# Attention into a routed expert layer: V splits, query/key halves, low parts and the router's last chunks moved in the order of the steps

## The chip, the cores and the metric

The kernel runs on one core of one Trainium2 chip. The metric is the device time of one execution in microseconds (us). TensorE (PE), VectorE (DVE), ScalarE (ACT), GpSimd (POOL) and SyncE (SP) each run their own instructions in order. SyncE only issues DMAs here, and GpSimd issues some.

## What is computed

Three stages follow each other. Cluster-masked attention over batch 2, 8 heads, 768 positions, 64 channels; then a router that sends each of the 1536 tokens (of 512 channels) to one of 8 experts; then a feed-forward layer of width 2048.

```python
    mask = q_assign[:, :, :, None] == k_assign[:, :, None, :]
    scores = scale * np.matmul(q, k.transpose(0, 1, 3, 2))
    scores = np.where(mask, scores, -1000000000.0)
    scores = scores - np.max(scores, axis=-1, keepdims=True)
    attn = np.exp(scores)
    attn = attn / (np.sum(attn, axis=-1, keepdims=True) + 1e-09)
    return np.matmul(attn, v).astype(np.float32)
...
    e_idx = np.argmax(logits, axis=1)
...
        h = np.maximum(x[mask] @ w1[e], 0.0)
        ye = h @ w2[e]
        out[mask] = gate_w[mask, None] * eom[mask, e, None] * ye
...
    h = x @ w_in
    g = h * (1.0 / (1.0 + np.exp(-h)))
    return (g @ w_out).astype(np.float32)
```

`q_assign` and `k_assign` are each position's nearest of 16 centroids.

## The kernel before

Attention is cut into 96 steps: 8 periods of 12. A period is one pair of heads of one batch entry, and its steps are 2 heads times 6 tiles of 128 queries. `run` goes through iterations i = 0, 1, 2, ... and writes each engine's instructions in the order of that loop; its last lines chain every instruction to the one before it on its engine, so that the order written is the order run.

Iteration i does this, in this order: the scores of step i + 1 (`qk_mm`, L371 and L373); what was deferred (`flush`: copies out of PSUM and DMAs); for a step i - 2 on TensorE its high part (`high`, ScalarE, L424); the softmax of step i (`soft`: VectorE's reduction L392, ScalarE's exponential L394, and, where the step is not on TensorE, the copy to 16 bits, L403); the eviction of a finished group of outputs (`out`, L469 to L471); the low part of a TensorE step i - 2 (`low2`, VectorE, L429); the transposes of a TensorE step i - 1 (`turn`, L418) or the low part of any other step i - 1 (`low`, GpSimd's subtraction L438); the first half of the tasks that are due in this round; up to two PVs (`pv`, L462 to L464, seven iterations behind their scores); the second half of the tasks; and one or two chunks of the router.

A probability tile is used as two 16-bit parts, high and low, and must be transposed. There are two ways. **TensorE steps** (chosen in `onpe`, in pairs) are transposed by TensorE into two PSUM tiles, from which ScalarE takes the high part and VectorE the low part. **The other steps** make both parts in SBUF, and for two steps together SyncE issues a DMA transpose (L442, tile pt). For steps 4, 5 and 8 of a period the 16-bit copy is VectorE's cast L437, which is written in `low`. PSUM tiles of `turn`, of the query/key transposes (L178), of the cluster scores (L193), of the masks and of the router share three banks.

**Tasks** come from a table of rounds in `plan` (round r is iteration r of the period; period 0 has its own rounds, marked z). They prepare the next pair's heads: transposes of queries and keys (`tr`), whose second halves are copied to other partitions by DMA (L298: QB from QA issued by GpSimd, KB from KA by SyncE); cluster scores and the best cluster (`sc`, and `best` in three pieces, L203 to L211, VectorE); masks (`m`: L338, L339, and four DMAs of SyncE, L342). They also split V into high and low (`split_v`, GpSimd, L152 to L156) and the queries and keys of the pair after the next (`halves`, ScalarE L330 and GpSimd L331).

SyncE issues, in the order of the loop, the loads of queries and keys (L169), the DMA transposes, the copies and stores of zeros (L1195). GpSimd also issues the router's scatters (L772). The router (`s.router`, L680 to L772) is a generator: one chunk of it is run in an iteration, a chunk that works on the PSUM banks only where no TensorE step needs them. Its part for a group of query tiles starts one iteration after the group's eviction was written (`late`). After the last step the rest of it is run without steps in between, and the first expert reads what was scattered (L905, tile xst to xt).

Of the kernel before, what the change touches and what calls it, by code (L numbers as in the profile page):

```python
# [30 lines left out]
class Att:  # L31
# [224 lines left out]
    def plan(s, pi, pairs, g0=None, vg=None):  # L256

        nc = s.nc
        u = []
        add = lambda r, f: u.append((r, f))  # L260
        nx = lambda g: lambda: next(g, None)
        if pi + 2 < len(pairs):
            add(3 if g0 else -1, lambda: s.load_qk(*pairs[pi + 2]))
        z = bool(g0)
        b, hp = pairs[pi]
        sp = lambda h, b=b, hp=hp: lambda: s.split_v(b, 2 * hp + h)
        if z:
            for r in (-1, 0, 0, 1, 1):
                add(r, nx(g0))
            for r in (3, 4, 4, 5, 6, 7, 8, 8):  # L270
                add(r, nx(vg))
        for h, r in enumerate((9, 10) if z else (-1, 0)):
            add(r, sp(h))
        if pi == 1:
            s.v1 = s.load_v(1)
        for r in {1: (3, 6, 10), 2: (6, 10), 3: (4, 5, 6, 6)}.get(pi, ()):
            add(r, nx(s.v1))
        if pi + 1 < len(pairs):
            b, hp = pairs[pi + 1]
            if z:  # L280
                for r in range(2):
                    add(r, lambda r=r: s.halves(pairs[1], r))
            hd = [None, None]
            ch = [None, None]
            oh = []

            def start(j):
                hd[j] = s.heads(2 * hp + j, j)
                if j == 0:
                    oh.append(s.ohp.tile([128, NT, 2, 2, C], BF16, tag='oh', name='oh'))  # L290

            def tr(j, a, half):
                if a == 0 and half == 0:
                    start(j)
                s.turned(hd[j][1 + 2 * a], s.nqk[b, hp][a], j, half, (-0.125, 1.0)[a])
                if half:
                    src, dst, e = ((hd[j][1][0:64], hd[j][2][0:64], nc.gpsimd), (hd[j][3][64:128], hd[j][4][0:64], nc.sync))[a]
                    s.defer.append(lambda: e.dma_start(dst.bitcast(F32), src.bitcast(F32)))  # L298

            def sc(j):  # L300
                s.scores(hd[j])
                ch[j] = s.best(s.clb, oh[0], j)
            bst = lambda j: lambda: next(ch[j])
            tr8 = [(j, a, half) for j in range(2) for a in range(2) for half in range(2)]
            for (j, a, half), r in zip(tr8, (2, 2, 3, 3, 4, 4, 5, 5) if z else (-1, -1, -1, 0, 0, 0, 3, 3)):
                add(r, lambda j=j, a=a, half=half: tr(j, a, half))
            for j, (r, r1, r2, r3) in enumerate(((4, 5, 6, 7), (6, 7, 8, 9)) if z else ((1, 2, 3, 4), (4, 5, 6, 7))):
                add(r, lambda j=j: sc(j))
                for q in (r1, r2, r3):
                    add(q, bst(j))  # L310

            def m():
                s.masks(oh[0], hd)
                for j in range(2):
                    s.ready[b, hp, j] = hd[j]
            add(9 if z else 8, m)
        if pi + 2 < len(pairs):
            for i, r in enumerate((5, 6) if not z else (9, 10)):
                add(r, lambda i=i: s.halves(pairs[pi + 2], i))
        u.sort(key=lambda x: x[0])  # L320
        return u
# [54 lines left out]
    def onpe(s, st):  # L376
        g = st['i'] // 2
        n = len(s.steps) // 2

        return (g % 3 == 0 and g >= 6) or g >= n - 6  # L380

    def dve(s, st):

# [65 lines left out]
    def pv(s, st):  # L449
        nc = s.nc  # L450
        b = st['b']
        h = st['hd'][0]
        t = st['t']
        pt = st['pt']
        g = st['g']
        gl = slice(g[0], g[-1] + 1)
        if t == g[0]:
            s.o = s.T('o2')[:, :NT * (D + 2)].rearrange('p (t d) -> p t d', t=NT) if st['j'] and st['pi'] == 7 and (g[-1] == NT - 1) else s.ps_o.tile([128, NT, D + 2], F32, tag='o', name='o')
        o = s.o
        vh, vl = s.vh[b, h]  # L460
        for kt in range(NT):
            nc.tensor.matmul(o[:, t, 0:D + 2], lhsT=pt[:, 0, kt], rhs=vh[:, kt], start=kt == 0, stop=False)  # L462
            nc.tensor.matmul(o[:, t, 0:D], lhsT=pt[:, 0, kt], rhs=vl[:, kt], start=False, stop=False)  # L463
            nc.tensor.matmul(o[:, t, 0:D + 2], lhsT=pt[:, 1, kt], rhs=vh[:, kt], start=False, stop=kt == NT - 1)  # L464
        if t == g[-1]:
            def ev():
                n = len(g)
                rs = s.sm.tile([128, NT], F32, tag='rs', name='rs')[:, :n]
                nc.vector.tensor_scalar(rs, o[:, gl, D], 1e-09, s.inv[b][:, 0, h:h + 1], op0=ALU.add, op1=ALU.mult)  # L469
                nc.vector.reciprocal(rs, rs)  # L470
                nc.vector.tensor_tensor(s.xb[b][:, gl, h * D:(h + 1) * D], o[:, gl, 0:D], rs.unsqueeze(2).to_broadcast([128, n, D]), op=ALU.mult)  # L471
                if h % 2 and s.router:
                    s.late.append((s.now + 1, b, h // 2, g))
            s.oev = ev

    def run(s):
# [36 lines left out]
        rg = []  # L513
        free = False
        n = len(steps)
        done = 0
        i = -1
        base = 0
        todo = []
        while done < n:  # L520
            s.now = i
            if i + 1 < n:
                st = steps[i + 1]
                if (i + 1) % (2 * NT) == 0:
                    base = i + 1
# [10 lines left out]
            if 0 <= i < n:  # L536
                s.soft(steps[i])
            s.out()
            if 2 <= i < n + 2 and s.onpe(steps[i - 2]):
                s.low2(steps[i - 2])  # L540
            if 1 <= i < n + 1:
                (s.turn if s.onpe(steps[i - 1]) else s.low)(steps[i - 1])
            now = []
            while todo and todo[0][0] <= i - base:
                now.append(todo.pop(0)[1])
            for f in now[:len(now) // 2]:
                f()
            for k in range(3 if i >= n - 12 else 2):
# [5 lines left out]
                f()  # L554
            if s.late and i >= s.late[0][0]:
                rg.append(s.router(s, *s.late.pop(0)[1:]))
            for k in range(2):
                if rg and (k == 0 or (i - base) % 12 == 9 and i < n - 12) and (free or not (1 <= i < n - 12 and s.onpe(steps[i - 1]))):
                    x = next(rg[0], 0)
                    free = x == 'free'  # L560
                    if x == 0:
                        rg.pop(0)
# [661 lines left out]
```

## Time and profile before

| | |
|---|---|
| Time, median of 3 runs | 864.39 us (862.42 to 864.69) |
| The profiled execution | 858.08 us, of which the span is 856.0 us |
| Mean granted TensorE clock in it | 0.925 |
| Busy: TensorE, VectorE, ScalarE, GpSimd | 749.6, 501.9, 415.2, 328.6 us |
| DMA | 117.09 MB, mean 137 GB/s |

The span runs from the first instruction to the last; the time has some 2 us around it. A busy share says how much of the span an engine worked, not whether it was waited for. Attention's steps take the first third of the span, the experts and the feed-forward layer the rest.

### The profile page before, as it was taken

What the parts mean: (1) busy time and instruction counts of PE and PEld (TensorE: products, weight loads), DVE (VectorE), ACT (ScalarE), POOL (GpSimd) and SP (SyncE); (2) the same over time, 40 slices, a digit from 0 to 9 for tenths busy, and PEclk for the clock granted to TensorE, in tenths of its full rate; (3) what the DMA queues carried; (4) which work ended last, traced back from release to release, by engine and by line L of the source; (5) the groups of instructions that cost most, each with busy time, mean ns of one, the idle gap of its engine ahead of it and who ended that gap; (6) DMA issues with size and microseconds to landing.
All of it is one profiled execution on the core that took longest, in us unless ns stands there. A gap on an engine that the chain in (4) does not pass through costs nothing.

```text
span 856.0 us, 14041 instructions
## 1 busy us (share of the span) xinstructions
PE 749.6 (88%) x5416; PEld 636.4 (74%) x5416; DVE 501.9 (59%) x905; ACT 415.2 (48%) x659; POOL 328.6 (38%) x271
## 2 busy tenths in 40 slices
PE   5859897869799873999899999889899999999994
PEld 4649787868788863888797887567688788878883
DVE  6757688567867777475555687699932322232221
ACT  3756777557485654565444654465522322222221
POOL 1678758385685316644333454335400000000000
PEclk9658999789799985999999999979999999999997
DMA  4399999696676536688664864465400100010001
GB/s 150 65 221 243 205 183 155 134 184 126 136 169 129 121 112 231 217 305 267 210 212 156 295 215 152 172 227 172 148 1 1 49 1 1 0 50 1 1 0 52
DMA packets 135752, 117.09 MB, mean 137 GB/s; under 512 B 100823, under 2 KB 106967, under 8 KB 135680
## 3 DMA queue, kind: packets, MB, share of 16 engines
q1 hardware_dynamic: 131728, 107.06, 48.0%
q0 software_dynamic: 3952, 9.08, 3.7%
q8 instruction: 44, 0.72, 0.4%
q14 instruction: 28, 0.23, 0.1%
HBM read 71.67 MB, written 18.45 MB: 105 GB/s over the span
## 4 chain that ended last, share of the span: by engine, by line
PE 33%; DMA 5%; issue 5%; DVE 4%; POOL 2%; ACT 1%; ACTq 0%; POOLq 0%; DVEq 0%
PE op L1146 13%; PE hp L1158 13%; PE yp L965 3%; DMA x<-ys,f 3%; PE hp L948 2%; POOL w L852 2%; PE hr L930 2%; DMA stage<-in_moe_w_out 1%; DVE stage L1091 1%; DVE stage L1092 1%; DVE stage L1090 1%; DMA stage<-in_moe_w_in 1%; DMA stage<-in_moe_w 1%; DMA out_x<-os 0%; ACT w L847 0%
## 5 line engine op out<-in xcount | busy, mean ns | idle before, releaser
L852 POOL TENSOR_TENSOR w<-stage,w 128x512 fp32r<-128x512 f32 (+1 forms) x54 | 102.2, 1898 | 117.6 <-ACT w L847 115.8
L1158 PE MATMUL hp<-XH,w 128*128 128x512 f32 x384 | 128.5, 406 | 6.8 <-DVE sg L1166 5.6
L847 ACT ACTIVATE w<-stage 128x1024 fp32r<-128x1024 f32 (+1 forms) x104 | 96.4, 940 | 62.4 <-DVE stage L1092 29.9
L438 POOL TENSOR_TENSOR p<-p,p 128x768 f16<-128x768 f32 x60 | 98.4, 1650 | 72.7 <-DVE p L437 42.3
L392 DVE TENSOR_REDUCE m<-sp 128x1 f32<-128x768 f32 x96 | 91.0, 952 | 44.4 <-PE sp L373 35.3
L394 ACT ACTIVATE p<-sp,m 128x768 f32<-128x768 f32 x96 | 86.6, 902 | 54.1 <-DVE m L392 49.3
L1146 PE MATMUL op<-w,GH 128*128 128x512 f32 x384 | 111.7, 397 | 0.0
L1166 DVE TENSOR_TENSOR sg<-hp,sg 128x512 f32<-128x512 f32 x48 | 33.1, 689 | 118.2 <-ACT sg L1165 118.2
L948 PEld LDWEIGHTS hp<-X,w 128*128 128x128 f32 x672 | 86.8, 190 | 11.4 <-DVE HL L951 7.7
L948 PE MATMUL hp<-X,w 128*128 128x256 f32 x672 | 90.0, 284 | 4.6 <-DVE HL L951 4.2
L1158 PEld LDWEIGHTS hp<-XH,w 128*128 128x128 f32 x384 | 73.9, 193 | 26.1 <-DVE sg L1166 7.2
L852 DVE TENSOR_TENSOR w<-stage,w 128x1024 fp32r<-128x1024 f32 x50 | 70.8, 1426 | 28.5 <-ACT w L847 25.1
L462 PE MATMUL o<-vh,pt 128*128 128x66 f16 x576 | 67.7, 202 | 22.2 <-DMA pt<-p 15.9
L1165 ACT ACTIVATE sg<-hp 128x512 f32<-128x512 f32 x48 | 28.6, 597 | 119.5 <-PE hp L1158 118.5
L1146 PEld LDWEIGHTS op<-w,GH 128*128 128x128 f32 x384 | 73.3, 191 | 17.5
L1158 PE MATMUL hp<-XL,w 128*128 128x512 f32 x192 | 77.6, 404 | 2.6 <-DVE XL L852 2.6
L462 PEld LDWEIGHTS <-pt 128*128 128x128 f16 x576 | 55.9, 102 | 29.8 <-DMA pt<-p 17.5
L371 PE MATMUL sp<-KA,QA 128*128 128x384 f32 x192 | 65.8, 426 | 11.8 <-ACT p L394 11.4
L463 PE MATMUL o<-vl,pt 128*128 128x64 f16 x576 | 67.1, 198 | 0.8 <-POOL vl L156 0.8
L1146 PE MATMUL op<-w,GL 128*128 128x512 f32 x192 | 67.0, 399 | 0.6 <-DVE GL L852 0.5
L464 PE MATMUL o<-vh,pt 128*128 128x66 f16 x576 | 66.9, 199 | 0.0
L965 PE MATMUL yp<-w,HH 128*128 128x512 f32 x224 | 63.7, 399 | 0.3 <-ACT HH L950 0.3
(206 smaller groups left out, 1447.2 us busy)
## 6 DMA issues: line engine op xcount, KB each, us to landing
stage<-in_moe_w SPq DMA_DIRECT2D x72, 512.0 KB, 4.7
stage<-in_moe_w_in SPq DMA_DIRECT2D x16, 512.0 KB, 4.7
stage<-in_moe_w_out SPq DMA_DIRECT2D x16, 512.0 KB, 3.5
xst<-z SPq DMA_DIRECT2D x16, 258.0 KB, 3.2
xt<-xst SPq DMA_DIRECT2D x7, 516.0 KB, 4.0
vt<-in_v SPq DMA_DIRECT2D x4, 768.0 KB, 7.2
xt<-x SPq DMA_DIRECT2D x6, 512.0 KB, 5.2
out_x<-os SPq DMA_DIRECT2D x12, 256.0 KB, 2.4
```

Source lines behind the costliest of these rows:

```text
L392: st['min'] = nc.vector.tensor_reduce(m, sv, axis=AX.XY, op=ALU.min).ins
L394: st['exp'] = nc.scalar.activation(p32, sv, AF.Exp, bias=m, scale=-1.0).ins
L438: s.nc.gpsimd.tensor_sub(p16[:, 1], p32, p16[:, 0])
L462: nc.tensor.matmul(o[:, t, 0:D + 2], lhsT=pt[:, 0, kt], rhs=vh[:, kt], start=kt == 0, stop=False)
L463: nc.tensor.matmul(o[:, t, 0:D], lhsT=pt[:, 0, kt], rhs=vl[:, kt], start=False, stop=False)
L464: nc.tensor.matmul(o[:, t, 0:D + 2], lhsT=pt[:, 1, kt], rhs=vh[:, kt], start=False, stop=kt == NT - 1)
L847: s.nc.scalar.activation(hi, src, AF.Copy)
L852: (eng or s.nc.vector).tensor_sub(lo, src, hi)
L948: nc.tensor.matmul(hp, lhsT=W1[k][w][:, f * 128:(f + 1) * 128], rhs=x[:, k, :N], start=n == 0, stop=n == 11)
L965: nc.tensor.matmul(yp, lhsT=h[:, f, i * 128:(i + 1) * 128], rhs=w, start=n == 0, stop=n == 23)
L1146: nc.tensor.matmul(op[i], lhsT=g[:, i * 128:(i + 1) * 128], rhs=w, start=f == 0 and m == 0, stop=f == 15 and m == 2)
L1158: nc.tensor.matmul(hp, lhsT=I[k, f // 8][w][:, fs], rhs=x[:, k], start=n == 0, stop=n == 11)
```

## The change

Numbers of rounds in the table of tasks are changed: in period 0 the pieces of loading V, the V splits, the second head's `best` and the halves; in all other periods the V splits go from rounds -1 and 0 to 1 and 2, and the halves from 5 and 6 to 7 and 8. `onpe` takes in one pair more, steps 6 and 7 (38 TensorE steps for 36, and 29 DMA transposes for 30). Where the step behind a TensorE step is not one itself, `low2` is written last of its iteration, as the last of the tasks. The router's part for the last evictions starts in the same iteration, and in the last iterations up to six of its chunks are run one behind the other, each with a flush.

```diff
@@ -267,9 +267,9 @@
         if z:
             for r in (-1, 0, 0, 1, 1):
                 add(r, nx(g0))
-            for r in (3, 4, 4, 5, 6, 7, 8, 8):
+            for r in (3, 3, 4, 4, 5, 6, 6, 6):
                 add(r, nx(vg))
-        for h, r in enumerate((9, 10) if z else (-1, 0)):
+        for h, r in enumerate((7, 9) if z else (1, 2)):
             add(r, sp(h))
         if pi == 1:
             s.v1 = s.load_v(1)
@@ -304,7 +304,7 @@
             tr8 = [(j, a, half) for j in range(2) for a in range(2) for half in range(2)]
             for (j, a, half), r in zip(tr8, (2, 2, 3, 3, 4, 4, 5, 5) if z else (-1, -1, -1, 0, 0, 0, 3, 3)):
                 add(r, lambda j=j, a=a, half=half: tr(j, a, half))
-            for j, (r, r1, r2, r3) in enumerate(((4, 5, 6, 7), (6, 7, 8, 9)) if z else ((1, 2, 3, 4), (4, 5, 6, 7))):
+            for j, (r, r1, r2, r3) in enumerate(((4, 5, 6, 7), (7, 8, 8, 9)) if z else ((1, 2, 3, 4), (4, 5, 6, 7))):
                 add(r, lambda j=j: sc(j))
                 for q in (r1, r2, r3):
                     add(q, bst(j))
@@ -315,7 +315,7 @@
                     s.ready[b, hp, j] = hd[j]
             add(9 if z else 8, m)
         if pi + 2 < len(pairs):
-            for i, r in enumerate((5, 6) if not z else (9, 10)):
+            for i, r in enumerate((7, 8) if not z else (8, 10)):
                 add(r, lambda i=i: s.halves(pairs[pi + 2], i))
         u.sort(key=lambda x: x[0])
         return u
@@ -377,7 +377,7 @@
         g = st['i'] // 2
         n = len(s.steps) // 2
 
-        return (g % 3 == 0 and g >= 6) or g >= n - 6
+        return (g % 3 == 0 and g > 0) or g >= n - 6
 
     def dve(s, st):
 
@@ -470,7 +470,7 @@
                 nc.vector.reciprocal(rs, rs)
                 nc.vector.tensor_tensor(s.xb[b][:, gl, h * D:(h + 1) * D], o[:, gl, 0:D], rs.unsqueeze(2).to_broadcast([128, n, D]), op=ALU.mult)
                 if h % 2 and s.router:
-                    s.late.append((s.now + 1, b, h // 2, g))
+                    s.late.append((s.now + (s.now < len(s.steps) - 2), b, h // 2, g))
             s.oev = ev
 
     def run(s):
@@ -536,13 +536,17 @@
             if 0 <= i < n:
                 s.soft(steps[i])
             s.out()
-            if 2 <= i < n + 2 and s.onpe(steps[i - 2]):
+            late = 2 <= i < n + 2 and s.onpe(steps[i - 2])
+            if late and (i - 1 >= n or s.onpe(steps[i - 1])):
                 s.low2(steps[i - 2])
+                late = False
             if 1 <= i < n + 1:
                 (s.turn if s.onpe(steps[i - 1]) else s.low)(steps[i - 1])
             now = []
             while todo and todo[0][0] <= i - base:
                 now.append(todo.pop(0)[1])
+            if late:
+                now.append(lambda st=steps[i - 2]: s.low2(st))
             for f in now[:len(now) // 2]:
                 f()
             for k in range(3 if i >= n - 12 else 2):
@@ -554,8 +558,10 @@
                 f()
             if s.late and i >= s.late[0][0]:
                 rg.append(s.router(s, *s.late.pop(0)[1:]))
-            for k in range(2):
-                if rg and (k == 0 or (i - base) % 12 == 9 and i < n - 12) and (free or not (1 <= i < n - 12 and s.onpe(steps[i - 1]))):
+            for k in range(2 if i < n - 2 else 6):
+                if i >= n - 2:
+                    s.flush()
+                if rg and (i >= n - 2 or k == 0 or (i - base) % 12 == 9 and i < n - 12) and (free or not (1 <= i < n - 12 and s.onpe(steps[i - 1]))):
                     x = next(rg[0], 0)
                     free = x == 'free'
                     if x == 0:
```

SyncE in period 0, before, from the transpose of steps 2 and 3 on (pt from p_404; p_463 is that of steps 4 and 5, p_533 of 6 and 7, p_593 of 8 and 9; the rows of L342 are the mask copies of the next pair):

```order
L442 DMA_TRANSPOSE pt<-p_404 128x24x128
L1195 DMA xst<-z 128x516
L298 DMA KB<-KA 64x768
L442 DMA_TRANSPOSE pt<-p_463 128x24x128
L1195 DMA xst<-z 128x516
L442 DMA_TRANSPOSE pt<-p_533 128x24x128
L1195 DMA xst<-z 128x516
L342 DMA QB<-mk 16x768
L342 DMA KB<-mk 16x768
L342 DMA QB<-mk 16x768
L342 DMA KB<-mk 16x768
L442 DMA_TRANSPOSE pt<-p_593 128x24x128
```

SyncE at the same place after the change (p_464 is the transpose of steps 4 and 5, p_607 of 8 and 9, and L1201 is the same store):

```order
L442 DMA_TRANSPOSE pt<-p_404 128x24x128
L1201 DMA xst<-z 128x516
L298 DMA KB<-KA 64x768
L442 DMA_TRANSPOSE pt<-p_464 128x24x128
L1201 DMA xst<-z 128x516
L342 DMA QB<-mk 16x768
L342 DMA KB<-mk 16x768
L342 DMA QB<-mk 16x768
L342 DMA KB<-mk 16x768
L442 DMA_TRANSPOSE pt<-p_607 128x24x128
```

The transpose of steps 6 and 7 and one store are gone from ahead of the four mask copies; the store comes behind the next transpose instead.

VectorE in rounds 7 to 9 of period 2, before (L392 the steps' reductions, L429 the low parts of the TensorE steps 6 and 7, L437 the cast of step 8):

```order
L392 TENSOR_REDUCE m<-sp 128x1
L429 TENSOR_TENSOR pt<-ptp,pt 128x384 x2
L392 TENSOR_REDUCE m<-sp 128x1
L429 TENSOR_TENSOR pt<-ptp,pt 128x384 x2
L437 CAST p_1752<-p_1750 128x768
L392 TENSOR_REDUCE m<-sp 128x1
```

The same place after:

```order
L392 TENSOR_REDUCE m<-sp 128x1
L429 TENSOR_TENSOR pt<-ptp,pt 128x384 x2
L392 TENSOR_REDUCE m<-sp 128x1
L437 CAST p_1767<-p_1765 128x768
L429 TENSOR_TENSOR pt<-ptp,pt 128x384 x2
L392 TENSOR_REDUCE m<-sp 128x1
```

The cast of step 8 now stands ahead of the low part of step 7.

GpSimd at the border of periods 2 and 3, before (L438 the low parts of steps 10 and 11, L152 to L156 a V split, L298 the copies of the second halves of the queries):

```order
L438 TENSOR_TENSOR p_1848<-p_1846,p_1848 128x768
L152 MEMSET vh 128x6x2
L154 TENSOR_SCALAR vt_339<-vt_339,vsc_597 128x384
L155 CAST vh<-vt_339 128x6x64
L156 TENSOR_TENSOR vl<-vt_339,vh 128x384
L298 DMA QB<-QA 64x768
L438 TENSOR_TENSOR p_1848<-p_1887,p_1848 128x768
L152 MEMSET vh 128x6x2
L154 TENSOR_SCALAR vt_339<-vt_339,vsc_597 128x384
L155 CAST vh<-vt_339 128x6x64
L156 TENSOR_TENSOR vl<-vt_339,vh 128x384
L298 DMA QB<-QA 64x768
```

The same place after:

```order
L438 TENSOR_TENSOR p_1865<-p_1863,p_1865 128x768
L298 DMA QB<-QA 64x768
L438 TENSOR_TENSOR p_1865<-p_1904,p_1865 128x768
L298 DMA QB<-QA 64x768
L152 MEMSET vh 128x6x2
L154 TENSOR_SCALAR vt_339<-vt_339,vsc_548 128x384
L155 CAST vh<-vt_339 128x6x64
L156 TENSOR_TENSOR vl<-vt_339,vh 128x384
L152 MEMSET vh 128x6x2
L154 TENSOR_SCALAR vt_339<-vt_339,vsc_548 128x384
L155 CAST vh<-vt_339 128x6x64
L156 TENSOR_TENSOR vl<-vt_339,vh 128x384
```

The two V splits stood before and behind the low part of step 11 and now stand together behind it; the second copy QB from QA comes ahead of both.

On ScalarE at the end of attention, the router's copy of 512 columns (L682) stood between the high parts of the last two steps, and its exponentials (L728, L739) behind them; these three now come ahead of both high parts.

## Rows read from the trace of the kernel before

**Rows 1.** The page, busy time and share of each engine.

```profile
PE 749.6 (88%) x5416; PEld 636.4 (74%) x5416; DVE 501.9 (59%) x905; ACT 415.2 (48%) x659; POOL 328.6 (38%) x271
```

**Rows 2.** Busy time by stretch: TensorE, its loads, VectorE, ScalarE, GpSimd; clock, DMA.

```profile
36.00:96.00 60.00, 46.70 (x499) 41.13 (x498) 42.22 (x82) 36.49 (x56) 44.66 (x39) 0.80 1.09 224
...
130.00:152.00 22.00, 15.11 (x198) 14.38 (x198) 16.59 (x32) 15.15 (x25) 18.98 (x19) 0.89 1.10 171
...
345.00:380.00 35.00, 34.62 (x229) 30.98 (x228) 21.79 (x29) 20.25 (x29) 20.30 (x12) 1.00 0.74 252
```

**Rows 3.** Timeline of TensorE: start, duration, line, count, idle time before.

```profile
62.56 0.98 PE L373 MATMUL sp<-KB,QB 80*128 80x384 f32 x2 [3.43 <-DMA KB<-mk]
...
151.81 0.24 PE L462 MATMUL o<-vh,pt 128*128 128x66 f16 x1 [6.84 <-DMA pt<-p]
...
190.77 0.24 PE L462 MATMUL o<-vh,pt 128*128 128x66 f16 x1 [7.29 <-DMA pt<-p]
...
230.78 0.62 PE L371 MATMUL sp<-KA,QA 128*128 128x384 f32 x2 [2.98 <-ACT p L394]
...
262.42 0.20 PE L462 MATMUL o<-vh,pt 128*128 128x66 f16 x1 [1.80 <-DMA pt<-p]
...
308.62 0.52 PE L418 MATMUL ptp<-ident,p 128*128 128x128 f32 x3 [1.18 <-DVE pt L429]
...
333.77 0.47 PE L905 MATMUL etp<-ident,xt 128*128 128x128 f32 x1 [13.01 <-DMA xt<-xst]
```

**Rows 4.** Timelines of SyncE and of ScalarE in period 0.

```profile
55.29 3.68 SPq L442 DMA_TRANSPOSE pt<-p  x1
...
59.68 0.59 SPq L342 DMA_DIRECT2D QB<-mk  x1
...
53.74 0.90 ACT L339 ACTIVATE mk<-mp,mcol 64x768 fp32r<-64x768 bf16 x1 [0.50 <-PE mp L338]
```

**Rows 5.** Groups of instructions in attention: count, busy time, mean ns, idle before.

```profile
L418 PE MATMUL ptp<-ident,p 128*128 128x128 f32 x216 | 32.8, 285 | 4.4 <-DVE pt L429 4.3
...
L206 DVE TENSOR_TENSOR cl<-cl,mx 128x192 f32<-128x192 f32 x14 | 5.1, 367 | 0.5
```

**Rows 6.** Timeline of SyncE at the border of periods 2 and 3.

```profile
130.22 4.32 SPq L442 DMA_TRANSPOSE pt<-p  x1
...
138.23 6.83 SPq L442 DMA_TRANSPOSE pt<-p  x1
```

**Rows 7.** Timelines of VectorE and of GpSimd there.

```profile
125.31 1.02 DVE L429 TENSOR_TENSOR pt<-ptp,pt 128x384 f16<-128x384 f32 x2 [1.61 <-ACT pt L424]
126.25 0.55 DVE L437 CAST p<-p 128x768 f16<-128x768 f32 x1
...
139.59 0.58 POOL L298 DMA_DIRECT2D QB<-QA  x1
```

**Rows 8.** Timelines of GpSimd and of SyncE at the border of periods 5 and 6.

```profile
249.00 0.12 POOL L152 MEMSET vh<- 128x12 f16 x1
...
252.48 1.67 POOL L438 TENSOR_TENSOR p<-p,p 128x768 f16<-128x768 f32 x1
...
254.18 3.62 SPq L442 DMA_TRANSPOSE pt<-p  x1
```

**Rows 9.** Timelines of VectorE and of GpSimd in the router's work.

```profile
226.54 1.67 DVE L757 TENSOR_TENSOR slot<-r_sl,r_sk 128x6 int32<-128x6 f32 x1
...
226.37 1.83 POOL L331 TENSOR_TENSOR nq<-qld,nq 128x768 fp32r<-128x768 f32 x1
```

**Rows 10.** Timelines of TensorE, VectorE and GpSimd at the end of attention.

```profile
315.85 0.23 PE L734 MATMUL rk<-moe_oh,ones 128*128 128x27 bf16 x3
...
315.92 0.29 DVE L471 TENSOR_TENSOR xb<-o,rs 128x128 f32<-128x128 f32 x1
...
321.96 0.17 DVE L761 RECIPROCAL xb<-r_g 128x2 f32<-128x2 f32 x1
...
326.74 0.98 POOL L772 DMA_INDIRECT xst<-xb,slot  x1 [0.30 <-issue]
```

## The prediction

> **What bounds the kernel now.** I read the busy shares first: TensorE is busy for 88% of the span, the three other compute engines for 38% to 59% [rows 1]. A share over the span hides two stages. Behind attention, with the experts, TensorE is full: 34.62 of 35 us at the full clock [rows 2]. Nothing that starts there can start earlier than attention ends, so what attention gains or loses is carried to the end nearly one for one. In attention TensorE is not full: from 36 to 96 us it works 46.70 of 60 us, from 130 to 152 us 15.11 of 22, with a granted clock of 0.80 and 0.89 and the DMA engines asked for more than they can move at once (share 1.09 and 1.10) [rows 2]. So the next view is TensorE's timeline, for its idle time and what ended it [rows 3]. The long waits are few: 3.43 us for the mask rows of the next keys (KB from mk), 6.84 and 7.29 us for a DMA transpose (pt), 2.98 us for an exponential, 1.80 us for another transpose, some of 1.18 us for a PSUM bank that VectorE's low part still reads, and 13.01 us ahead of the first expert. The change is worth what it takes from these.
>
> The sum is made against the profiled execution (856.0 us of span, 858.08 in all). The median is 864.39, 6.31 above; I take the difference as the same on both sides and subtract the sum from the median.
>
> **1. Steps 6 and 7 go to TensorE (period 0).** SyncE issues one DMA transpose less. The one that goes took SyncE 3.68 us from 55.29, directly ahead of one store and the four mask copies, the first at 59.68 [rows 4]. Those copies are what TensorE waits for until 62.56 [rows 3]. Without the transpose the first copy may be issued at 55.29, 4.39 us earlier; its source is written by ScalarE from 53.74 to 54.64 [rows 4], so that doesn't hold it. Added are 12 transposes on TensorE, four copies on ScalarE, four subtractions on VectorE; two conversions on ScalarE and two subtractions on GpSimd go. Twelve at 0.285 us of the group's mean [rows 5] are 3.4 us of TensorE, beside 13.3 us of idle time in that stretch (60 less 46.70) [rows 2]: hidden, if they fall before the wait. I take the whole wait, -3.4. The bounds: -1.0 if 2.4 of the 3.4 us added to TensorE fall on the path, and -4.4 if the 4.39 us carry through.
>
> **2. V split and second QB copy, periods 2 and 3.** Both long waits are for the transpose of the period's steps 10 and 11. In the first it was issued at 138.23, the one ahead of it, of steps 8 and 9, at 130.22 [rows 6], and TensorE went on at 151.81 [rows 3]. Two things move. First, the cast of step 8 went behind two low parts, which waited 1.61 us for ScalarE: low parts 125.31, cast 126.25 [rows 7]. Now it goes ahead of them, and can start when VectorE's row before is done, near 123.7. GpSimd's chain of steps 8 and 9 then starts earlier, but step 9 also needs ScalarE's conversion, which doesn't move; what is left for the transpose is 1.2 us by my count (issue 129.0 for 130.22). Second, the two V splits left from between GpSimd's subtractions, and the second QB copy, issued at 139.59 while the transpose was on its way [rows 7], goes out some 5 us earlier (two splits, 2.9 us each by part 3). It moves 64x768 floats, 0.197 MB, which is 1.15 us at the 171 GB/s of that stretch [rows 2]; I credit 0.8. Together -2.0 for each place, -4.0 for two. From below, 0: the transpose of steps 10 and 11 waits for SyncE, which has two loads and a copy ahead of it, not for GpSimd. From above, -14.1: both waits go.
>
> The Trainium skill, "DMA: Bandwidth & Descriptors", section "Queues, rings and completion order", says that a DMA engine takes packets of its queue rows in turn, and that one row's ring is consumed in order. By it the transposes stay behind SyncE's loads however early GpSimd is done, and this part would be nearer to 0 than to -14.1; the trace agrees in so far as the loads stand ahead and the wait is there, and no row shows the turn-taking.
>
> **3. Period 5 to 6.** The subtraction of step 11 started at 252.48, and its transpose was issued at 254.18 right behind it. Ahead of it stood a V split from 249.00 [rows 8]. The split and the copy behind it took 3.48 us (252.48 less 249.00), of which a copy is 0.58 [rows 7]; only the copy stays ahead. The transpose, which nothing else holds, goes 2.9 us earlier, and TensorE's 1.80 us at 262.42 [rows 3] go: -1.8.
>
> **4. The halves in period 5.** The router's 128x6 instruction L757 took 1.67 us at 226.54, beside GpSimd's 1.83 us half at 226.37; both ended at 228.2 [rows 9]. The next reduction was late, and TensorE stood 2.98 us for the exponential [rows 3]. The halves go two rounds later, the router stays. I take -1.5, the held VectorE time of 1.67 less its own short work; bounds 0 and -2.98.
>
> **5. Late low parts.** For 13 pairs the second step's two subtractions come behind the tasks of their iteration. A PSUM bank of the shared three then comes free later. In round 3 two passes of best stand ahead (the one shown takes 0.37 us, the other about as long, 0.74 together), in round 9 the 0.55 us cast [rows 5, 7]. All of it on the path would be 6 x 0.74 + 7 x 0.55 = 8.3 us. Before, such waits are 4.3 us over 18 pairs, 0.24 each [rows 5]; six more like it are +1.4, I take +1.5. From below 0, as TensorE has other work.
>
> **6. The router's last parts.** They now run without a pause, but the last group's scatters need the last PV. TensorE's router work on the group before, whose ranks ended at 316.08 (315.85 + 0.23), goes ahead of the last step's transposes and PV. Behind it come the transposes, two copies and two low parts at some 0.5 us each (a pair took 1.02 [rows 7]), the PV and hand-overs, some 3 us: the last PV ends near 319.2. Its eviction, then some 0.9 us, ends near 320.1, and from there to the last xb it was 5.9 us (316.21 to 322.13): 326.0. The last of six scatters was issued at 326.74 [rows 10]; with two left behind 326.0, 1.4 us apart, it comes at 327.7, and the read that TensorE waits for until 333.77 [rows 3] goes with it: +1.0. Bounds: -3.0 (the ranks end earlier than I count and the scatters come closer together) and +2.5 (the hand-overs take 1.5 us more).
>
> Sum: -3.4 - 4.0 - 1.8 - 1.5 + 1.5 + 1.0 = **-8.2**: 849.9 for the profiled execution, and 864.39 - 8.2 = **856.2**. What a measurement here tells from no change is about 0.3%, 2.6 us: faster is below 861.8, slower above 867.0.
>
> **Rivals.**
> A (forecast): parts 1 to 6 as above, 852 to 860. Chance 0.48.
> B: the long waits go. If the transpose lands in time once its place in the DMA traffic is earlier, part 2 is -14.1 and the sum -18.3: 846. For it: each wait is for one landing, and what is asked of the DMA engines in that stretch is only 10% above what they carry. Against it: SyncE's queue order. 0.16.
> C: the next queue takes the gain. SyncE and the DMA engines are full in these stretches, so a transpose that starts earlier lands no earlier. Part 1 gives its lower bound 1.0, part 2 nothing: -1.0 - 1.8 - 1.5 + 1.5 + 1.0 = -1.8: 862.6. For it: shares of 1.09 and 1.10. Against it: in the first of these stretches one transpose less is asked for, and in the others the second QB copy no longer runs beside one. 0.19.
> D, the other sign: the late low parts hold the banks. The priced wait is the 1.18 us at 308.62 [rows 3]; at each of 13 places 15.3 us, in place of the +1.5: 856.2 - 1.5 + 15.3 = 870.0. The gains without this term are 9.7 us, so it ends slower than before from 9.7 / 13 = 0.75 us a place, and measurably so from 0.95. Against it: the work put ahead of them takes only 0.55 to 0.74 us, and TensorE has PVs to do. 0.09.
> E: GpSimd's halves now meet VectorE's cast of step 8. Held for a whole 1.83 us half [rows 9] in five periods: +9.1: 865.3, no change. Against it: the half waits for ScalarE, and cast and half may miss each other. 0.06. The Trainium skill, "SBUF — State Buffer", section "Who interferes with whom", has it that a cast or scalar operation of VectorE can take the port pair shared with GpSimd, and then one blocks the other for a whole instruction; the common end in rows 9 agrees with it, and by it E would come each time the two meet.
> F: nothing moves, 864. 0.02.
>
> **Chances and range.** Faster: A, B and a quarter of C, 0.48 + 0.16 + 0.05 = 0.69. Same: the rest of C, E and F, 0.14 + 0.06 + 0.02 = 0.22. Slower: D, 0.09. For 8 in 10 the range leaves out D and the lower half of B: 846 to 865, which holds A, C, E, F and half of B, 0.83. A's own range is 852 to 860.
>
> **What would show it.** Part 1: no 3.4 us wait for KB near 62 us, and SyncE's first mask copy about 4 us earlier behind the second QK copy. Part 2: the cast of step 8 directly behind a reduction, the transpose of steps 8 and 9 issued about 1.2 us earlier in the period, and waits for pt that are 2 us shorter; gone would mean B, unchanged C. Part 3: no wait for pt at the end of period 5. Part 4: L757's successor at some 0.2 us and no wait for an exponential there. Part 5: TensorE's waits for VectorE's low parts in the sum near 6 us, not 15. Part 6: TensorE's wait ahead of the first expert ends later relative to the last reduction by about 1 us. I would be wrong if a wait not listed here grows, above all in the periods after those with a gain, whose transposes then meet other loads.

## The result

The changed kernel took 859.86 us (median of 20 runs, 849.56 to 866.51), the kernel before 865.44 us beside it (20 runs, 860.78 to 873.72). The ratio is 0.990 with an interval of 0.9872 to 0.9927: 8.7 us faster (6.3 to 11.1). The forecast was 8.2 us faster. The ratio leaves out executions more than 1.5% above the fastest of their kernel, among them the profiled one of 865.18 us (the medians, over all executions, lie 5.6 us apart), so the span of that profile is not set against the one of before; its stages are.

The page, busy times of the changed kernel:

```profile
PE 760.4 (88%) x5428; PEld 644.1 (75%) x5428; DVE 501.3 (58%) x909; ACT 413.9 (48%) x661; POOL 329.1 (38%) x269
```

The stretches, columns as in [rows 2], and one from 246 us on:

```profile
36.00:96.00 60.00, 49.41 (x518) 44.44 (x519) 46.24 (x88) 38.34 (x61) 44.03 (x39) 0.86 1.01 206
130.00:152.00 22.00, 20.01 (x239) 18.43 (x238) 17.53 (x36) 13.74 (x23) 16.31 (x16) 0.88 1.10 210
246.00:260.00 14.00, 13.53 (x110) 12.61 (x111) 5.36 (x11) 1.80 (x2) 6.94 (x5) 0.52 0.67 123
```

TensorE works 20.01 of 22 us where it worked 15.11, with the DMA engines as much asked for as before (1.10). The third row is new: TensorE is hardly idle, and is granted about half its clock.

TensorE's timeline at its waits, in the order of [rows 3]:

```profile
62.65 0.59 PE L373 MATMUL sp<-KB,QB 80*128 80x384 f32 x2 [2.47 <-DMA QB<-mk]
...
147.23 0.23 PE L462 MATMUL o<-vh,pt 128*128 128x66 f16 x1 [1.80 <-DMA pt<-p]
...
180.42 0.20 PE L462 MATMUL o<-vh,pt 128*128 128x66 f16 x1 [2.57 <-DMA pt<-p]
...
220.41 0.62 PE L371 MATMUL sp<-KA,QA 128*128 128x384 f32 x2 [1.31 <-ACT p L394]
...
246.47 0.23 PE L462 MATMUL o<-vh,pt 128*128 128x66 f16 x1 [2.12 <-DMA pt<-p]
...
303.15 0.52 PE L418 MATMUL ptp<-ident,p 128*128 128x128 f32 x3 [1.18 <-DVE pt L429]
...
331.89 0.48 PE L911 MATMUL etp<-ident,xt 128*128 128x128 f32 x1 [10.72 <-DMA xt<-xst]
```

The two long waits for a transpose went from 6.84 and 7.29 us to 1.80 and 2.57. The wait at 246.47 is not that of 262.42 moved: it is for the transpose of steps 8 and 9, one pair earlier, and the stretch at half clock of the table above follows it.

The other places that the forecast named: VectorE's first reduction, its cast of step 8, and the router's instruction of [rows 9] (L763 now); then SyncE's first mask copy and the two transposes of [rows 6]; then TensorE's transposes, all in attention:

```profile
26.49 0.96 DVE L392 TENSOR_REDUCE m<-sp 128x1 f32<-128x768 f32 x1
...
123.33 0.95 DVE L392 TENSOR_REDUCE m<-sp 128x1 f32<-128x768 f32 x1
124.19 0.55 DVE L437 CAST p<-p 128x768 f16<-128x768 f32 x1
125.40 1.02 DVE L429 TENSOR_TENSOR pt<-ptp,pt 128x384 f16<-128x384 f32 x2 [0.65 <-ACT pt L424]
...
217.62 0.17 DVE L763 TENSOR_TENSOR slot<-r_sl,r_sk 128x6 int32<-128x6 f32 x1
```

```profile
58.44 0.59 SPq L342 DMA_DIRECT2D QB<-mk  x1
...
129.69 4.28 SPq L442 DMA_TRANSPOSE pt<-p  x1
...
136.90 8.27 SPq L442 DMA_TRANSPOSE pt<-p  x1
```

```profile
L418 PE MATMUL ptp<-ident,p 128*128 128x128 f32 x228 | 36.5, 292 | 6.7 <-DVE pt L429 6.2 <-DVE r_e L751 0.3
```

The end of attention, VectorE's last reduction and last eviction, and GpSimd's last two scatters:

```profile
300.44 0.96 DVE L392 TENSOR_REDUCE m<-sp 128x1 f32<-128x768 f32 x1 [0.55 <-PE sp L373]
...
316.12 0.22 DVE L469 TENSOR_SCALAR rs<-o,vsc 128x2 f32<-128x2 f32 x1 [2.74 <-remote]
```

```profile
322.81 1.76 POOL L778 DMA_INDIRECT xst<-xb,slot  x1 [6.09 <-DVE o_cnt L800]
324.88 0.98 POOL L778 DMA_INDIRECT xst<-xb,slot  x1 [0.31 <-issue]
```

From VectorE's first reduction to its last the steps took 273.95 us (300.44 less 26.49), before 281.95: 8.0 less. From the last reduction to the first expert's transposes it was 31.45 us (331.89 less 300.44), before 27.86: 3.6 more. From there to the end it was 531.4 us, before 522.3: 9.1 more, although the diff touches nothing there. And the first reduction came 2.5 us later (26.49 for 23.96; it lies between 23.96 and 26.91 in all fourteen traces, at 24.48 in the second one of the changed kernel). So in this trace what the steps gain is lost again behind them.

### The profile page after: what moved, and what is told of

Read it like the earlier page. It is cut to its first block, busy times and chain, and to the rows that moved or that the text cites. A ratio compares the mean times of both kernels' runs of the same rounds, so it can differ in the third digit from the quotient of the medians.

```text
span 863.3 us, 14073 instructions
## 1 busy us (share of the span) xinstructions
PE 760.4 (88%) x5428; PEld 644.1 (75%) x5428; DVE 501.3 (58%) x909; ACT 413.9 (48%) x661; POOL 329.1 (38%) x269
## 4 chain that ended last, share of the span: by engine, by line
PE 34%; DMA 6%; issue 4%; DVE 3%; POOL 2%; ACT 1%; ACTq 0%; POOLq 0%; DVEq 0%
PE op L1152 13%; PE hp L1164 13%; PE yp L971 3%; PE hp L954 2%; DMA x<-ys,f 2%; PE hr L936 2%; POOL w L858 2%; DMA stage<-in_moe_w_out 2%; DMA stage<-in_moe_w_in 1%; DVE stage L1096 1%; DVE stage L1097 1%; DMA out_x<-os 0%; DMA stage<-in_moe_w 0%; DVE w L858 0%; DVE stage L1098 0%
## 5 line engine op out<-in xcount | busy, mean ns | idle before, releaser
L853 ACT ACTIVATE w<-stage 128x1024 fp32r<-128x1024 f32 (+1 forms) x104 | 96.2, 940 | 58.5 <-DMA stage<-in_moe_w 24.7
L392 DVE TENSOR_REDUCE m<-sp 128x1 f32<-128x768 f32 x96 | 91.4, 952 | 33.5 <-PE sp L373 29.6
L438 POOL TENSOR_TENSOR p<-p,p 128x768 f16<-128x768 f32 x58 | 95.3, 1650 | 32.5 <-DVE p L437 27.2
L954 PE MATMUL hp<-X,w 128*128 128x256 f32 x672 | 91.8, 287 | 5.4 <-DVE HL L957 5.3
L1164 PEld LDWEIGHTS hp<-XH,w 128*128 128x128 f32 x384 | 74.1, 193 | 29.2 <-DVE sg L1172 10.4
```

The costliest lines, as they stand in the source:

```text
L392: st['min'] = nc.vector.tensor_reduce(m, sv, axis=AX.XY, op=ALU.min).ins
L438: s.nc.gpsimd.tensor_sub(p16[:, 1], p32, p16[:, 0])
L853: s.nc.scalar.activation(hi, src, AF.Copy)
L954: nc.tensor.matmul(hp, lhsT=W1[k][w][:, f * 128:(f + 1) * 128], rhs=x[:, k, :N], start=n == 0, stop=n == 11)
L1164: nc.tensor.matmul(hp, lhsT=I[k, f // 8][w][:, fs], rhs=x[:, k], start=n == 0, stop=n == 11)
```

## The experiments

Ratios are to the kernel before on the same chip. e1 to e4 ran on one chip, e5 to e8 on a second, e9 to e12 on a third. "Steps", "tail" and "rest" are the stretches from the first reduction to the last, from there to the first expert, and from there to the end.

**e1, the changed kernel again.** No edit.

> The changed kernel once more, nothing left out. In its first trace the steps took 273.95 us from the first reduction to the last (before: 281.95), the first expert started 31.45 us behind the last reduction (before: 27.86), and the rest took 531.4 us (before: 522.3). Theory: the shorter steps (about -8) come again, the tail again costs 3 to 4 us, and the 9 us of the rest are chance: 520 to 526 now. Rival: the rest is slower because the kernel is changed (its first loads and weights meet the later scatters): again near 531.

Ratio 0.9921 (0.9886 to 0.9957). Steps 261.15 us, tail 30.72, rest 536.3. The longer tail came again, and so did the long rest, as the rival had it. The rest is 529.6 to 536.9 us in six traces: the three of the changed kernel (the first, e1, e9), e2, e3 and e4. It is 521.2 to 524.8 us in the eight others: two of the kernel before, e5, e6, e7, e10, e11 and e12. All seven traces with the halves in their old rounds are among these eight; of the seven with moved halves only e5 is. What differs in the rest is shown at e10. Why the steps are so short in e1 (273.95 and 274.40 us in the other two traces of this kernel) stays open. So stages are compared on one chip where they can be.

**e2, without the row of router chunks.**

```diff
-                    s.late.append((s.now + (s.now < len(s.steps) - 2), b, h // 2, g))
+                    s.late.append((s.now + 1, b, h // 2, g))
...
-            for k in range(2 if i < n - 2 else 6):
-                if i >= n - 2:
-                    s.flush()
-                if rg and (i >= n - 2 or k == 0 or
+            for k in range(2):
+                if rg and (k == 0 or
```

> The router's last parts as before (one iteration later, no row of chunks), everything else of the change kept. Theory: the row of chunks puts the last PV behind the router's work on the group before, so without it the first expert starts 27 to 28.5 us behind the last reduction instead of 31.45: 3 us less in all, ratio to the kernel before near 0.986 where the changed kernel has 0.990. Rival: the 2 us that VectorE stood ahead of the last eviction with TensorE done were chance, and the order costs only the 1.0 us forecast: no difference that the times show.

Ratio 0.9882 (0.9832 to 0.9931), tail 26.59 us. The tail is 4.1 us shorter than in e1, the ratio 0.0039 lower, which is inside the intervals: the times decide neither for the theory nor for the rival.

**e3, the V splits back in their rounds.**

```diff
-        for h, r in enumerate((7, 9) if z else (1, 2)):
+        for h, r in enumerate((7, 9) if z else (-1, 0)):
```

> V splits of periods 1 to 7 back in rounds -1 and 0, everything else of the change kept. Theory: the shorter waits for the transpose of steps 10 and 11 in periods 3 and 4 (6.84 to 1.80 us, 7.29 to 2.57 us) come from the splits, which left from between GpSimd's low parts and from ahead of the second QB copy: now both are 5 us or more again, and the steps take about 280 us. Rival: they come from VectorE's cast of step 8 ahead of the low parts: both stay under 3 us and the steps take about 274 us.

Ratio 1.0023 (0.9986 to 1.0059): the gain is gone. TensorE's timeline, its longest waits for a transpose:

```profile
118.06 0.24 PE L462 MATMUL o<-vh,pt 128*128 128x66 f16 x1 [5.21 <-DMA pt<-p]
...
151.88 0.24 PE L462 MATMUL o<-vh,pt 128*128 128x66 f16 x1 [4.21 <-DMA pt<-p]
```

The third, at 185 us, is 1.61 us; in e1 the three were 0.91, 1.06 and 3.28. So the waits grow by 5.8 us in all and the steps by 11.2 (272.35 for 261.15). That speaks for the splits, though not with the 5 us at both places that was expected, and the steps are nearer to the rival's 274 us than to my 280; the first trace and e9, with the splits moved, take no less (273.95 and 274.40). What shows the worth of the splits is the times: the intervals of e1 and e3 don't meet.

**e4, the late low parts back.**

```diff
-            if late and (i - 1 >= n or s.onpe(steps[i - 1])):
+            if late:
```

> The low part of the second TensorE step of a pair back ahead of the iteration's tasks, everything else of the change kept. Theory: this is worth little: the cast of step 8 goes behind two low parts again, its pair's transpose is issued 1 us later, and TensorE's waits for VectorE's low parts hardly change (+1.5 forecast for the late order): steps 273 to 276 us. Rival: the cast's earlier place is the gain: waits for the transpose of steps 10 and 11 of 5 us or more in periods 3 and 4, steps of about 280 us.

Ratio 0.9971 (0.9932 to 1.0011), steps 273.64 us against e1's 261.15, and waits of 4.34 us at 83.84 and 4.62 at 186.25 for transposes. The steps came out as in my theory, but the waits are partly the rival's, and the ratio is 0.0050 above e1's, with intervals that overlap. e12 asks again what the order is worth.

**e5, without the pair of steps 6 and 7.**

```diff
-        return (g % 3 == 0 and g > 0) or g >= n - 6
+        return (g % 3 == 0 and g >= 6) or g >= n - 6
```

> Steps 6 and 7 of period 0 off TensorE again (36 TensorE steps, 30 DMA transposes), everything else of the change kept. In the two traces of the changed kernel TensorE still waited 2.47 and 2.65 us for the mask rows of period 1, and period 0 took 36.8 and 37.1 us against 39.7 before. Theory: the pair is worth those 2.7 us and little else: period 0 takes 39 to 40 us, steps 2 to 4 us longer, ratio to the kernel before 0.994 to 0.996. Rival: the pair is worth nothing, since the transpose that goes only lets SyncE wait for the mask: period 0 at 37 us, ratio 0.991.

Ratio 0.9956 (0.9915 to 0.9998). Period 0 took 39.9 us; with the pair it was 36.0 to 37.1 in eight traces (38.4 in e4), before 39.7 and 39.6. TensorE's wait for the mask rows:

```profile
65.04 0.66 PE L373 MATMUL sp<-KB,QB 80*128 80x384 f32 x1 [4.05 <-DMA KB<-mk]
```

With the pair this wait was 1.68 to 2.65 us in nine traces. The pair is worth some 3 us of period 0, as in my theory, and the wait shortens by 1.4 to 2.4 us only.

**e6, the splits alone in the kernel before.**

```diff
-        for h, r in enumerate((9, 10) if z else (-1, 0)):
+        for h, r in enumerate((9, 10) if z else (1, 2)):
```

> The kernel before with one edit: the V splits of periods 1 to 7 in rounds 1 and 2. Without them the changed kernel was at a ratio of 1.0023. Theory: the splits carry the gain by themselves: ratio 0.988 to 0.993, waits for the transpose of steps 10 and 11 in periods 3 and 4 of 1.5 to 3.5 us for 6.84 and 7.29. Rival: they gain only together with the late low parts (their removal gave 0.9971), since each shortens the same chain of GpSimd: ratio 0.995 to 1.0.

Ratio 0.9894 (0.9834 to 0.9954), as much as the whole change (0.990). TensorE at the two places of part 2:

```profile
155.02 0.24 PE L462 MATMUL o<-vh,pt 128*128 128x66 f16 x1 [4.03 <-DMA pt<-p]
...
190.71 0.23 PE L462 MATMUL o<-vh,pt 128*128 128x66 f16 x1 [4.41 <-DMA pt<-p]
```

The ratio is the one expected, the waits are longer than the 1.5 to 3.5 us expected, and the steps are only 4.0 us shorter than before (277.98 for 281.95). The trace thus places less than half of the 9.1 us that the ratio makes of 861.89.

**e7 and e10, the halves back in rounds 5 and 6.**

```diff
-            for i, r in enumerate((7, 8) if not z else (8, 10)):
+            for i, r in enumerate((5, 6) if not z else (8, 10)):
```

> The halves of periods 1 to 5 back in rounds 5 and 6, everything else of the change kept. Theory: they cost where a router instruction of VectorE runs beside one (period 5, 1.67 us) and where they stand between GpSimd's low parts: a wait of about 3 us for an exponential in period 5 is back, ratio 0.992 to 0.995. Rival: nothing, the wait was that one trace's: ratio 0.990 to 0.992, and VectorE's short instruction is as short.

Ratio 0.9811 (0.9768 to 0.9854). Both expectations fell: without this part the change gains twice as much. e9 and e10 put the two on one chip.

**e8, the kernel before again.**

> The kernel before once more, nothing changed. In its first trace the rest behind the first expert's start took 522.3 us, in five traces with the change or most of it 531 to 537. Theory: part of the gain of the steps is given back there, because the first weights are not converted further when attention ends earlier: 520 to 525 again. Rival: that trace was a good one in this stretch, as its 858.08 lies 7 us below the median of its kernel: 530 to 535 now, and about 310 us up to the first expert.

860.74 us, steps 282.10, tail 27.66, rest 524.8: my theory of a gain given back in the rest had this on its side, but e7's rest was 521.5 us with an earlier end of attention, so an earlier end alone doesn't lengthen the rest. Of the waits of [rows 3] those of 6.43 and 6.56 us are there, and the 1.80 us one at the end of period 5 is not (0.31).

**e9, the changed kernel beside e10.** No edit.

> The changed kernel on one chip with the three that follow, nothing left out: ratio 0.989 to 0.993, as twice before (0.9900 and 0.9921). In period 5 the transpose of steps 8 and 9 is issued 11.9 us behind the reduction of step 8, as in its other traces.

Ratio 0.9927 (0.9892 to 0.9962).

> The kernel with the halves of periods 1 to 5 back in rounds 5 and 6, again. Theory: its 0.9811 against 0.9900 and 0.9921 is the halves' cost, which the moved halves take in period 5, where GpSimd also issues the router's scatters: the transpose of steps 8 and 9 is issued 9.9 us behind the reduction of step 8 instead of 11.9. The ratio is again below the changed kernel's by 0.006 to 0.010, and there is no wait for that transpose. Rival: it was the chip of that call: the two ratios differ by less than 0.004.

Ratio 0.9820 (0.9765 to 0.9875): 0.0107 below e9, 9.2 us of the 859.87 us of the kernel before there (the medians, 855.02 and 846.94, differ by 8.1). So the moved halves cost some 9 us. GpSimd's timeline in period 5 of e9 (L331 the halves, L778 the scatters, L438 the low parts of steps 8 and 9), and the same of e10:

```profile
224.69 1.81 POOL L331 TENSOR_TENSOR nq<-qld,nq 128x768 fp32r<-128x768 f32 x1 [0.33 <-ACT nq L330]
...
227.71 2.05 POOL L331 TENSOR_TENSOR nk<-kld,nk 128x768 fp32r<-128x768 f32 x1
229.92 0.99 POOL L778 DMA_INDIRECT xst<-xb,slot  x1 [0.16 <-issue]
230.93 1.67 POOL L438 TENSOR_TENSOR p<-p,p 128x768 f16<-128x768 f32 x1
...
235.05 1.68 POOL L438 TENSOR_TENSOR p<-p,p 128x768 f16<-128x768 f32 x1
```

```profile
222.01 1.83 POOL L331 TENSOR_TENSOR nk<-kld,nk 128x768 fp32r<-128x768 f32 x1
...
227.90 1.67 POOL L438 TENSOR_TENSOR p<-p,p 128x768 f16<-128x768 f32 x1
...
232.03 1.66 POOL L438 TENSOR_TENSOR p<-p,p 128x768 f16<-128x768 f32 x1
```

In e9 the halves run around and behind the reduction of step 8 (224.9), ahead of the low part that the transpose waits for; that transpose is issued 11.9 us behind the reduction, in e10 9.9 us. TensorE in e9 then waits for it; in e10 there is no such wait. Periods 5 and 6 of e9, then of e10 (columns as in [rows 2]):

```profile
246.82 0.20 PE L462 MATMUL o<-vh,pt 128*128 128x66 f16 x1 [1.69 <-DMA pt<-p]
```

```profile
198.00:233.50 35.50, 28.55 (x322) 24.82 (x321) 25.14 (x62) 22.31 (x37) 24.32 (x23) 0.86 0.79 154
233.50:271.40 37.90, 35.87 (x385) 32.69 (x384) 23.62 (x47) 22.57 (x38) 23.75 (x23) 0.82 0.70 131
```

```profile
195.60:232.80 37.20, 31.70 (x322) 28.04 (x321) 25.48 (x62) 22.34 (x37) 26.17 (x25) 0.77 0.70 154
232.80:264.00 31.20, 29.77 (x386) 26.91 (x385) 23.44 (x47) 22.64 (x38) 21.76 (x21) 1.00 0.76 148
```

Period 5 is longer in e10, at the lower clock (0.77 for 0.86); period 6 is 6.7 us longer in e9, at 0.82 for 1.00. Periods 5 and 6 together took 73.4 us in e9 (74.8 in the first trace, 73.6 in e5) and 68.4 in e10 (69.5 in e7, 68.8 before). So 5 us of the difference between these two traces are in this place. The wait doesn't come each time: in e1 to e4 the transpose is issued as late, TensorE waits at most 0.7 us for it, and the two periods take 65.5 to 69.7.

More of the difference lies behind attention. The first expert starts at 330.78 us in e9 and at 323.53 in e10, 7.3 us apart, and from there to the end e9 takes 529.6 us and e10 521.2, 8.4 more (the traced execution of e9 took 862.27 us, above the median of 855.02). In two more pairs that differ in the line of the halves alone, on different chips, all of it is there: e1 and e2, with moved halves, start the first expert earlier than e7 and e11 (316.35 for 323.52, 318.22 for 320.23), and their rests are 14.8 and 13.5 us longer.

The rest is the same work, but not in the same order. That the order written is the order run holds for attention and router only, since the chain in `run` holds no other instructions. Those of the experts are left to the scheduler that the kernel's last lines turn on (`schedule_with_timeline_sim=True`), and an edit in the table of tasks can change the order that comes out. ScalarE behind the first expert's start, in e9 and then in e10 (L853 copies X or converts weights w, L956 writes the hidden values HH):

```profile
340.24 0.60 ACT L853 ACTIVATE X<-etp 128x512 fp32r<-128x512 f32 x1
342.58 0.38 ACT L956 ACTIVATE HH<-hp 128x256 fp32r<-128x256 f32 x1 [1.74 <-PE hp L954]
342.86 1.05 ACT L853 ACTIVATE w<-stage 128x1024 fp32r<-128x1024 f32 x1
```

```profile
330.70 0.60 ACT L853 ACTIVATE X<-etp 128x512 fp32r<-128x512 f32 x1
331.63 1.06 ACT L853 ACTIVATE w<-stage 128x1024 fp32r<-128x1024 f32 x1 [0.34 <-DMA stage<-in_moe_w]
333.04 0.38 ACT L956 ACTIVATE HH<-hp 128x256 fp32r<-128x256 f32 x1 [0.35 <-PE hp L954]
```

All engines have one and the same order there in the changed kernel and e4 (rest 529.6 to 536.3 us), another in the kernel before and e6 (522.3 to 524.8), a third in e7 and e10 (521.5 and 521.2). So a good part of what the halves cost may be this order and not their place in GpSimd's queue. No run changes the order alone, so neither is shown as the cause; and e5, with moved halves and an order of its own, has a rest of 522.0 us.

**e11, neither halves nor row of chunks**: the edits of e2 and e7 together.

> As the one ahead of it, and the router's last parts as before too. Theory: the row of chunks costs some 3 us at the first expert's start (31 us behind the last reduction with it, 26.6 without), so this is the fastest of all, 0.003 below the one ahead of it, near 0.978 where that is near 0.981. Rival: the tail's saving is inside the spread: the same ratio within 0.003.

Ratio 0.9823 (0.9782 to 0.9863), tail 27.71 us against e10's 30.41. The times don't show these 2.7 us: the rival stands. 846.50 us against 846.94, both 13 us below the kernel before.

**e12, the late low parts alone in the kernel before**: the lines of `run` with `late`.

> The kernel before with one edit: the low part of a pair's second TensorE step is written last of its iteration. The forecast had +1.5 us for it, the removal from the changed kernel gave 0.9971 for 0.9921. Theory: it is a gain by itself, since the cast of step 8 comes ahead: the transpose of steps 8 and 9 is issued some 8.2 us behind the reduction of step 8 instead of 9.3, ratio 0.993 to 0.997. Rival, the forecast's: late banks cost 0 to 8 us: ratio 1.000 to 1.008, with waits for VectorE's low parts grown from 4 us in all.

Ratio 0.9888 (0.9848 to 0.9928), a larger gain than expected. TensorE at the two places of part 2:

```profile
155.21 0.24 PE L462 MATMUL o<-vh,pt 128*128 128x66 f16 x1 [3.23 <-DMA pt<-p]
...
188.44 0.20 PE L462 MATMUL o<-vh,pt 128*128 128x66 f16 x1 [2.13 <-DMA pt<-p]
```

The transpose of steps 8 and 9 is issued 8.1 to 8.8 us behind the reduction of step 8 in periods 1 to 4 (9.3 to 10.4 before), and TensorE's waits for VectorE's low parts are 4.7 us in all. The steps took 276.92 us, 5.0 less than before, about half of what the ratio says.

## Why the prediction was right

The sign was right, the main mechanism too (TensorE's waits for transposes in attention get shorter), and the number came out; but that it came so near is luck, as two errors of some 9 us cancelled. With the halves in their old rounds the change gains 15.5 us (e10, 0.0180 of 859.87) to 16.3 (e7, 0.0189 of 861.89): all parts but part 4 were forecast at -6.7 and brought about -16. The moved halves, forecast at -1.5, cost some 9. Nor did it hold that what attention gains is carried to the end nearly one for one: from the first expert's start to the end the three traces of the changed kernel take 4.9 to 14.0 us more than the two of the kernel before. One slip stands in the range: rival E's 865.3 is counted as held by 846 to 865 and lies just outside.

**Part 1, -3.4: right in size.** Period 0 is 2.6 to 3.7 us shorter in eight traces with the pair, and not in e5, which lacks it. The mask copy is issued 31.95 us behind the first reduction (58.44 less 26.49) where it was 35.72 (59.68 less 23.96): 3.8 us earlier of the 4.39. But the wait didn't vanish as I had it; it is 2.47 us, since TensorE comes to it earlier.

**Part 2, -4.0: the mechanism right, the size too small.** The cast stands directly behind a reduction, at 124.19, and the transpose of steps 8 and 9 is issued 8.1 us behind the reduction of step 8 instead of 9.3: the 1.2 us forecast. The waits fell from 14.1 us (13.0 in e8) to 4.4 (4.3 in e1, 4.4 in e9): 8.6 to 9.8 us, well towards the bound of 14.1 and rival B. The step that was mis-sized is the 0.8 us credited to the DMA traffic. From the issue of the transpose of steps 10 and 11 to TensorE's read of it were 13.6 us (138.23 to 151.81) and are 10.3 (136.90 to 147.23): 3.3 us less on the way, beside the 1.2 us of the issue. Splits alone (e6) leave 8.4 us of the 14.1, the cast alone (e12) 5.4; why the way itself gets shorter in e12 too, where the second QB copy did not move ahead of the splits, is not settled. The rule from the Trainium skill's "DMA: Bandwidth & Descriptors", "Queues, rings and completion order", as I read it, would have had this part near 0; the rows decide otherwise: the loads stand ahead of the transpose as before, and it lands sooner all the same.

**Part 3, -1.8: failed.** The wait that it took away was one trace's: 0.31 us in e8. Near its place came, in three of the seven traces with moved halves (the first, e5, e9), a wait of 1.7 to 2.1 us for the transpose of steps 8 and 9, and half the clock for some 13 us.

**Part 4, -1.5: failed.** The wait fell from 2.98 to 1.31 us, about as forecast, and L763 took 0.17 us. But that is not the halves' doing, whose move costs some 9 us: with the halves in their old rounds both are as short, the wait is 1.05 us in e7 and e10, and the instruction in e7, shortest, median, longest in ns, is

```profile
L763 DVE TENSOR_TENSOR slot<-r_sl,r_sk x3: 163/165/166, 217.8 to 312.4; 128x6 int32<-128x6 f32 x1, 128x4 int32<-128x4 f32 x1, 128x2 int32<-128x2 f32 x1
```

Nor did that instruction make the wait: in e12 it took 0.17 us, and the wait is 2.95 us all the same (in e6 1.65 and 3.73). What shortens the wait is not shown.

**Part 5, +1.5: right as a cost, wrong as a part.** The waits for the low parts went from 4.3 to 6.2 us, as forecast, and rival D fell. But I put the gain of this order, the cast that it lets pass, into part 2 at 1.2 us a place; alone the order is worth 9.6 us (0.0112 of 859.87). Parts 2 and 5 together were forecast at -2.5, and each of their edits brings more than 9 us by itself (e6, e12); what the two bring together without the rest of the change was not run.

**Part 6, +1.0: too small in the trace.** The tail is 29.61 to 31.45 us in eight traces with the row of chunks, 27.86 and 27.66 before, 26.59 and 27.71 without the row: some 2 to 4 us. In the first trace the last scatter came 24.44 us behind the last reduction (324.88 less 300.44) where it was 20.83; I had 21.8. VectorE's 2.74 us ahead of the last eviction have no cause in the profile.

**What I had not counted:** the halves. Their cost of some 9 us is the price of rival E, but not its mechanism: VectorE's casts average 821 ns in the changed kernel and 820 in e10, where the halves are back. In period 5 the halves took a place in GpSimd's queue between a reduction and the low part of its step, and behind attention the order of the experts' instructions changed with them. I asked what the moved halves would meet on VectorE, not what stands behind them on GpSimd, and I took the stage behind attention as unchanged. How the 9 us divide between the two is open.

## What to carry to other kernels

Ask of every moved instruction what stands behind it in its own engine's queue, and who waits for that: the same edit that frees one transpose here (splits) delays another when it is made to the halves (11.9 us for 9.9). Compare the order of the instructions behind the edited stage as well: where a scheduler sets it, an edit in one stage can reorder the next. When a change of many parts gains, try it without each part: one line fewer was worth as much again as the whole change. And don't add up the gains of parts tried alone: two edits of 1.1% each, and a pair worth some 3 us, gave 1.8 to 1.9% together, which the intervals don't tell from their sum or from less.

## What was not expected of the hardware

A wait of 1.7 to 2.1 us was followed by some 13 us at a granted clock of 0.50 to 0.55 in three traces (the first, e5 and e9), in which TensorE was busy nearly all the time. The wait need not be the cause: e10, which hasn't got it, is granted 0.77 in period 5, less than e9 there (0.86). And the stretch behind the first expert's start, the same work in all fourteen traces though not in one order, took 521 to 537 us, a difference larger than what the whole change is worth. The long ones show it from their start: over the first 20 us TensorE is busy for 14.2 to 19.1 us in the six long ones and for 19.44 in each of the eight short ones, and over the first 60 us the granted clock averages 0.86 to 0.93 in the long ones and 0.95 to 0.97 in the short ones.
